# Block 5's first layer by seven products, batch 0 mixed by channel blocks, and values of batch 0 loaded packed, in an attention and low-rank mixer kernel

## The chip, the cores and the metric

The kernel runs on one core of a Trainium2 chip. The metric is the device time of one execution in microseconds (us). Engines are named as in the profile: PE is TensorE (PEld its weight loads), DVE VectorE, ACT ScalarE, POOL GpSimd, SP SyncE. SP, ACT and POOL also issue DMAs; 16 DMA engines move the data of all three.

## The reference

Eight batches of attention with 8 heads of 64 channels, 576 queries, and 592 keys of which the first 16 are "beacons" that every query sees; behind it a mixer over tokens of rank 32, and a two-layer network with ReLU over channels, with a residual:

```python
k_all = np.concatenate([beacon_k, k], axis=2)
v_all = np.concatenate([beacon_v, v], axis=2)
scores = scale * np.matmul(q, k_all.transpose(0, 1, 3, 2))
causal[:, Nb:] = np.triu(np.ones((S, S), dtype=bool), k=1)
scores = np.where(causal, -1000000000.0, scores)
a = np.exp(scores - scores.max(-1, keepdims=True))
a /= a.sum(-1, keepdims=True) + 1e-09
x = np.matmul(a, v_all).transpose(0, 2, 1, 3).reshape(B, S, H * D)
h = x.transpose(0, 2, 1) @ U @ V
u = x + h.transpose(0, 2, 1)
out = u + np.maximum(u @ w_ch1, 0.0) @ w_ch2
```

U is 576x32, V is 32x576, w_ch1 is 512x2048, w_ch2 is 2048x512. All matmuls run in float16 with sums in float32.

## The kernel before

**The work.** Attention goes by pairs of heads: pair p is batch p // 4, heads 2(p % 4) and the next, so there are 32 pairs. The keys and queries of a pair are regrouped on chip (`pr`), turned so that channels lie on partitions (`kT`, `qT`; by PE through a PSUM tile `tps` and two copies, or from batch 3 on by a DMA that transposes, `raw`, and one copy that reorders), and multiplied in four visits a to d (`sps`); after each visit ACT takes the exponential of both heads (`expt`, L321). DVE masks them (L304), PE multiplies with the values `vs` (`po`, 15 matmuls a head, L331), and DVE divides (L340) into `xb`. When the four pairs of a batch are done, the mixer takes `xb`: a product with U (`qtp`, `qts`), then one with V added to x turned, which gives `uT`, channels on partitions, tokens along the row. In the first batches PE turns x by multiplying with the identity (`ups`, L390), later a DMA does (`xt`, L351).

**The blocks.** The 4608 tokens of `uT` go through the network in nine blocks of 512, 0 to 8, which don't line up with the batches of 576: block 0 needs batch 0 alone, block 5 batches 4 and 5, block 8 batch 7. The first layer of a block is 16 chunks of 128 hidden channels (`g_unit`, tile `gps`, L529): four matmuls of 512 columns, one for each 128 input channels cc, and a ReLU into `gT`. Blocks 6, 7 and 8 use instead Strassen's scheme of seven half-sized products (`first_product`, L566): 28 steps of four matmuls of 256 columns, whose sums go by ACT into float32 tiles `hP` (L109) and by DVE into `gT` (L581), after sums of tokens (`token_sum`, `tb`/`tc`) and of weights (`first_sum`, `wf`). The second layer (`product`, L620) has seven products in all blocks; its operands `sT` are sums and differences of quarters of `gT` (`operand_sum`, L601). The scheme needs the second column half of the first eight chunks with the first half taken off; DVE does that while it moves each chunk out of PSUM (L534, and L583 in the seven-product blocks). The result is added to the turned tokens `ut` (transposed by DMA, L520) by DVE (L645) and stored.

**The order.** No scheduler moves anything: `SCRIPT` is a list of some 960 short words, each engine gets the instructions of the words in that order, and each engine's queue runs strictly in order. So a word late in the list can't overtake one before it on the same engine. The words: `G` regroup, `H` cast head rows, `T` turn (the letters that follow name k or q and the engine that copies), `S` a visit of scores and its exponentials, `M` mask, `A` values, `X` mixer, `g` chunk, `F` first-layer product, `V`, `N` and `W` sums of tokens and weights, `p` operand sum, `P` second-layer product, `U`, `x`, `R` transposes by DMA, `k q b v w` loads issued by POOL, and `I1`, one filler matmul of 512 columns on the identity (`idle`, L241). Tiles in PSUM come from one ring of eight, so PE can run at most eight tiles ahead of the engines that empty them. The first loads of batch 0's keys and queries (`load_first`: tiles `stm`, `sth`) are issued by SP and ACT ahead of the list, in float32, and cast on chip.

## Time and profile before

| | |
|---|---|
| median of 3 runs | 341.67 us (340.97 to 342.67) |
| the profiled execution | 341.91 us, of which its span 340.3 us |
| around the span | 1.6 us |
| granted PE clock, mean | 0.999 |
| POOL busy | 103.6 us, 30% of the span |
| DMA moved | 44.17 MB in 135600 packets, 108384 of them under 512 bytes |

The span runs from the first to the last instruction. A busy share counts an instruction from its start to its end; matmuls overlap, so a PE that is always busy can still hold fillers or matmuls that run slower. What one matmul costs is read from how many stand in a stretch of the chain of waits that has no break.

### The profile page before, as it was taken

Reading aid. Unit: us, or ns where it says so; the run is one execution under the profiler, and the core shown is the slowest. Engines: PE = TensorE matmul, PEld = TensorE weight load, DVE = VectorE, ACT = ScalarE, POOL = GpSimd, SP = SyncE. Lnnn points to the kernel's source line nnn. Section 1 sums busy time; section 2 is a strip of 40 time slices with the busy share of each in tenths; the row PEclk is TensorE's granted clock in tenths of the full one; section 3 lists DMA queues with packets and bytes.
Section 4 is the critical chain, followed back from the end, with each engine's and each line's share of the span. In section 5 each row is a group of like instructions: output and inputs, shape, how many; then the busy total and the mean of one; then the engine's idle time right before and its main releaser. Section 6 shows DMA issues by size and latency. Waiting matters only on the chain.

```text
span 340.3 us, 8963 instructions
## 1 busy us (share of the span) xinstructions
PE 330.1 (97%) x3527; PEld 227.9 (67%) x3527; DVE 263.4 (77%) x681; ACT 228.3 (67%) x495; POOL 103.6 (30%) x137
## 2 busy tenths in 40 slices
PE   6989999999999999999999999999999999999994
PEld 2456555684668755775577646765688888888883
DVE  3489687994869766984888768885999999896872
ACT  3779987849787889878886798267912842544500
POOL 7787673070530802360015220000001503303300
PEclk9999999999999999999999999999999999999999
DMA  8999999999999998999969998463445501203023
GB/s 170 237 188 167 126 184 197 118 127 213 159 163 189 163 203 127 128 148 191 183 95 145 175 174 115 33 161 99 48 63 159 85 13 63 77 3 94 3 80 128
DMA packets 135600, 44.17 MB, mean 130 GB/s; under 512 B 108384, under 2 KB 130912, under 8 KB 135552
## 3 DMA queue, kind: packets, MB, share of 16 engines
q0 software_dynamic: 69008, 17.54, 60.1%
q1 hardware_dynamic: 65952, 25.66, 39.9%
q8 instruction: 29, 0.48, 0.6%
q10 hardware_dynamic: 592, 0.34, 0.3%
q14 instruction: 19, 0.16, 0.2%
HBM read 37.63 MB, written 9.44 MB: 138 GB/s over the span
## 4 chain that ended last, share of the span: by engine, by line
PE 84%; DVE 10%; issue 2%; ACT 1%; DMA 1%; ACTq 0%; DVEq 0%
PE gps L529 25%; PE cpY L620 17%; PE cpD L620 9%; PE sps L316 8%; PE po L331 8%; PE cpA L620 4%; PE fpY L566 3%; DVE gT L581 3%; PE idle L241 2%; PE tps L263 2%; PE fpD L566 2%; DVE sT L601 1%; DVE ob L645 1%; DMA sth<-in_beacon_k_dram 1%; PE ups L397 1%
## 5 line engine op out<-in xcount | busy, mean ns | idle before, releaser
L321 ACT ACTIVATE expt<-sps 128x496 f16<-128x496 f32 (+2 forms) x256 | 111.6, 543 | 13.4 <-PE sps L316 11.9
L529 PE MATMUL gps<-uT,w 128*128 128x512 f16 x384 | 91.8, 380 | 0.0
L620 PEld LDWEIGHTS <-gT 128*128 128x128 f16 x576 | 54.6, 98 | 10.5 <-issue 2.3
L529 PEld LDWEIGHTS <-w 128*128 128x128 f16 x384 | 34.3, 98 | 37.1 <-issue 2.4
L587 POOL TENSOR_SCALAR gT<-gT 128x512 f16<-128x512 f16 x12 | 17.8, 1493 | 105.7 <-DVE gT L581 89.1
L620 PEld LDWEIGHTS <-sT 128*128 128x128 f16 x432 | 40.8, 98 | 8.0 <-issue 2.0
L203 POOL DMA_DIRECT2D vs<-in_v_dram x50 | 40.8, 838 | 3.8 <-DMA w<-in_moe_w_ch_dram 1.7
L304 DVE TENSOR_TENSOR expt<-expt,bigmask 128x512 f16<-128x512 f16 x64 | 26.9, 421 | 18.8 <-ACT expt L321 18.8
L331 PEld LDWEIGHTS <-expt 128*128 128x128 f16 (+1 forms) x960 | 35.2, 98 | 8.7 <-DVE expt L304 1.1
L539 ACT ACTIVATE gT<-gps 128x512 f16<-128x512 f32 x48 | 29.3, 618 | 15.4 <-PE gps L529 14.9
L331 PE MATMUL po<-vs,expt 128*128 128x65 f16 (+1 forms) x960 | 37.8, 194 | 0.7 <-DVE expt L304 0.6
L620 PE MATMUL cpY<-wsum,gT 128*128 128x256 f16 x288 | 36.1, 273 | 0.0
L620 PE MATMUL cpD<-w,sT 128*128 128x256 f16 x288 | 35.6, 273 | 0.3 <-DVE sT L601 0.3
L316 PE MATMUL sps<-qT,kT 64*128 64x80 f16 (+4 forms) x384 | 34.3, 284 | 0.2 <-DVE qT L265 0.2
L340 DVE TENSOR_TENSOR xb<-po,rec 128x320 f16<-128x320 f32 x64 | 31.5, 492 | 2.2
L534 DVE SCALAR_TENSOR_TENSOR gT<-gps,gT 128x256 f16<-128x256 f32 x48 | 19.7, 420 | 13.0 <-ACT gT L533 12.9
L109 ACT ACTIVATE hP<-fpY 128x512 f32<-128x512 f32 x24 | 13.7, 597 | 23.1 <-PE fpY L566 22.0
L533 ACT ACTIVATE gT<-gps 128x256 f16<-128x256 f32 x48 | 18.9, 412 | 12.2 <-PE gps L529 11.9
L316 PEld LDWEIGHTS <-kT 64*128 64x128 f16 x384 | 13.8, 94 | 19.8 <-issue 11.1
L645 DVE TENSOR_TENSOR ob<-cpY,ut 128x512 f32<-128x512 f32 (+1 forms) x28 | 18.7, 667 | 5.9 <-PE cpY L620 5.9
L566 PEld LDWEIGHTS <-wf 128*128 128x128 f16 x192 | 18.6, 98 | 3.1 <-issue 0.7
L620 PE MATMUL cpY<-w,gT 128*128 128x256 f16 x144 | 17.7, 273 | 0.0
(118 smaller groups left out, 484.7 us busy)
## 6 DMA issues: line engine op xcount, KB each, us to landing
out_dram<-ob SPq DMA_DIRECT2D x16, 512.0 KB, 4.7
st<-in_k_dram POOLq DMA_DIRECT2D x6, 512.0 KB, 8.0
st<-in_q_dram POOLq DMA_DIRECT2D x6, 512.0 KB, 8.3
vs<-in_v_dram POOLq DMA_DIRECT2D x18, 128.0 KB, 7.9
w<-in_moe_w_ch_dram POOLq DMA_DIRECT2D x4, 512.0 KB, 7.5
w<-in_moe_w_ch_dram POOLq DMA_DIRECT2D x2, 1024.0 KB, 12.0
stm<-in_k_dram SPq DMA_DIRECT2D x4, 256.0 KB, 6.0
out_dram<-ob SPq DMA_DIRECT2D x4, 256.0 KB, 2.8
```

Of the source, the lines that this page charges most:

```text
L203: nc.gpsimd.dma_start(out=dst[a : a + nq[j], j, :, :], in_=src[hs, ds(q0[j], nq[j]), :].rearrange("h p d -> p h d"))
L304: nc.vector.tensor_tensor(out=e4, in0=e4, in1=bigmask, op=ALU.min)
L316: nc.tensor.matmul(ps[i][:, ds(o, w)], kT[hp, c, ds(P * ch, P)], qT[hp, c, ds(qa, w)], start=True, stop=True,)
L321: nc.scalar.activation(out=ex[i][:, ds(PAD + SLOT * g, gw[g])], in_=ps[i][:, 0 : gw[g]], func=AF.Exp, scale=scale)
L331: nc.tensor.matmul(po[:, j, :], ex[0 : nk[c], ds(blk[(c, j)], P)], vs[0 : nk[c], ds(c * H * E + h * E, E)], start=(c == 0), stop=(c == j),)
L340: nc.vector.tensor_tensor(out=xb[:, h // 2, :, ds(D * (h % 2), D)], in0=po[:, :, 0:D], in1=r.broadcast_to([P, NT, D]), op=ALU.mult)
L529: nc.tensor.matmul(g, w1[:, cc, ts(dc, P)], uT[:, cc, ds(ring(t0), 512)], start=(cc == 0), stop=(cc == NCC - 1))
L534: nc.vector.scalar_tensor_tensor(out=gT[:, dc, H2:512], in0=g[:, H2:512], scalar=0.0, in1=gT[:, dc, 0:H2], op0=ALU.max, op1=ALU.subtract,)
L539: nc.scalar.activation(out=gT[:, dc, :], in_=g, func=AF.Relu)
L566: nc.tensor.matmul(ps[:, i, :], a[:, kk, ts(2 * mp + i, P)], b[:, kk, :], start=opens and i == 0 and kk == 0, stop=kk == 1, skip_group_che ...
L620: nc.tensor.matmul(ps[:, i, :], a[:, f, ds(P * i, P)], b[:, f, :], start=opens and i == 0 and f == 0, stop=f == NK - 1, skip_group_check=True,
L645: nc.vector.tensor_tensor(out=out, in0=ps[:, ii, :], in1=other, op=ALU.add)
```

## The change

- **Block 5's first layer** joins blocks 6 to 8 in the seven products: 64 matmuls of 512 columns become 112 of 256.
- **Values of batch 0** (`f`, `packed_loads`): rows 112 to 575 come in one DMA of four tokens per packet into a tile `vf`, the first 112 rows and the beacons in two more, instead of 12 DMAs of one token per packet. PE then picks the rows apart (`D`, `unpack`): four matmuls of 512 columns with a selecting matrix `pick` for each of four key blocks, and a copy into `vs`.
- **Batch 0 is mixed by channel blocks** (`j`, `J`): each cc as soon as its pair of heads is done, its matmuls standing alone instead of four side by side. **Chunks begun ahead** (`h`): four chunks of block 0 issue three of their four matmuls before the fourth channel block stands.
- **Joint turns**: transposes of `uT` and `xb` take two channel blocks in one DMA (18 for 36, and 10 for 20). `uT` is laid out block by block, and every batch's mixer is cut where a block ends.
- **Bulk differences**: every chunk goes out by one ReLU of 512 columns on ACT; DVE takes the first half off in one instruction of 1024 elements per half of the chunks, at `p..0`.
- **ReLU by engine**: in the seven-product blocks the script names the engine (A, V, G) of each ReLU that follows a DVE sum.
- **The script is written anew.** POOL now regroups 24 half pairs from float16 tiles and 5 from float32 (1 and 2 before), and reorders 19 of the transposed tiles (none before). The fillers `I1` go from 37 to 24. The last second-layer products stand in the same order.

The core of the diff:

```diff
+    def packed_loads(src, bsrc, vs, vf):
+        dst = vs[:, :].rearrange("p (c h e) -> p c h e", h=H, e=E)[:, 0, :, 0:D]
+        np_ = (S - nq[0]) // VJ
+        nc.gpsimd.dma_start(
+            out=vf[0:np_], in_=src[:, nq[0] : S, :].rearrange("h (p j) d -> p h (j d)", j=VJ)
+        )
+        nc.gpsimd.dma_start(out=dst[Nb : Nb + nq[0]], in_=src[:, 0 : nq[0], :].rearrange("h p d -> p h d"))
+        beacon_load(nc.gpsimd, bsrc, dst, ALLH)
+
+    def unpack(vf, vs, c, copy):
+        ps = pst([P, H, D], F32, name="vps")
+        n = nq[c]
+        rows = ds(VG * (c - 1), n // VJ)
+        for j in range(VJ):
+            nc.tensor.matmul(
+                ps[0:n], pick[rows, ds(VJ - 1 - j, n)], vf[rows, :, ds(D * j, D)], start=(j == 0), stop=(j == VJ - 1)
+            )
+        copy(out=vs[0:n, :].rearrange("p (c h e) -> p c h e", h=H, e=E)[:, c, :, 0:D], in_=ps[0:n])
...
-        edge = NBR * 512 - ring(u0)
-        cuts = [0, edge if 64 <= edge < S else q0[2], S]
+        cuts = [0, 512 - u0 % 512, S]
...
+        def part_of(cc, copy):
+            rs = ds(R * cc, R)
+            for a, e in zip(cuts, cuts[1:]):
+                n = e - a
+                ups = pst([P, n], F32, name="ups")
...
+                nc.tensor.matmul(
+                    ups, cell["q"][rs, :], Vsb[rs, ds(a, n)], start=False, stop=True, skip_group_check=True
+                )
+                copy(out=ring(u0 + a)[:, cc, ds((u0 + a) % 512, n)], in_=ups)
...
-            if dc < NK:
-                nc.scalar.activation(out=gT[:, dc, 0:H2], in_=g[:, 0:H2], func=AF.Relu)
-                nc.vector.scalar_tensor_tensor(
-                    out=gT[:, dc, H2:512], in0=g[:, H2:512], scalar=0.0, in1=gT[:, dc, 0:H2],
-                    op0=ALU.max, op1=ALU.subtract,
-                )
-            else:
-                nc.scalar.activation(out=gT[:, dc, :], in_=g, func=AF.Relu)
+            if n is not None:
+                begun[dc] = g, n
+                return
+            nc.scalar.activation(out=gT[:, dc, :], in_=g, func=AF.Relu)
...
-                if n == 3:
-                    nc.vector.scalar_tensor_tensor(
-                        out=n3, in0=n3, scalar=0.0, in1=a11, op0=ALU.max, op1=ALU.subtract
-                    )
-                elif n == 2:
-                    nc.gpsimd.tensor_scalar_max(out=out, in0=out, scalar1=0.0)
-                else:
-                    nc.scalar.activation(out=out, in_=out, func=AF.Relu)
+                RELU[eng](out)
...
+            if j == 0:
+                nc.vector.tensor_tensor(out=n3, in0=n3, in1=a11, op=ALU.subtract)
...
-        B I1 GqA0 HqA0 I1 I1 I1 k1A I1 b1 I1 HkV0 GkV0 TkV0 v0A TqA0 Sa0:3 I1 GqG1 u I1 GkV1 TkV1 GkA4
...
+        GqV0 I1 HkA0 I1 u HqV0 B f0 I1 I1 I1 I1 I1 GkG0 I1 I1 TqV0 I1 I1 q1B I1 I1 I1 TkV0 Sc0 I1 s I1
+        Sd0 GkG1 Sa0:3 Sb0 M0.0 M0.1 k1A I1 TkV1 GqG1 DV3 DV4 GkA2 DA2 TqA1 I1 DV1 I1 GqA2 Sd1 b1 Sb1
...
```

**The opening on POOL.** First the rows of POOL's queue behind the constants, in the kernel before (`st`, `hd` are loads of batch 1, `vs` values, `pr` the regrouped pairs of batch 0):

```order
L196 DMA st_191<-in_k_dram 128x4x256
L190 DMA hd_189<-in_k_dram 64x4x64
L193 DMA hd_189<-in_beacon_k_dram 16x8x64
L193 DMA vs_126<-in_beacon_v_dram 16x4x64
L203 DMA vs_126<-in_v_dram 112x4x64
L203 DMA vs_126<-in_v_dram 128x4x64 x3
L203 DMA vs_126<-in_v_dram 80x4x64
L253 CAST pr<-stm 128x512
L741 CAST hd_142<-sth 80x128
```

and in the changed kernel:

```order
L220 DMA vf<-in_v_dram 116x8x256
L223 DMA vs_127<-in_v_dram 112x8x64
L203 DMA vs_127<-in_beacon_v_dram 16x8x64
L282 CAST pr<-stm 128x512
L206 DMA st_234<-in_q_dram 128x4x256
L200 DMA hd_232<-in_q_dram 80x4x64
L282 CAST pr<-stm 128x512
L822 CAST hd_142<-sth 80x128
L206 DMA st_233<-in_k_dram 128x4x256
L200 DMA hd_231<-in_k_dram 64x4x64
L282 CAST pr<-stm 128x512
L822 CAST hd_143<-sth 80x128
```

The packed values now stand first, ahead of every load of batch 1, and casts of the first pairs stand between the loads.

**The packed values on PE.** PE's queue where the turn of pair 1's queries ends, before (`tps` the turned tile, `sps` scores):

```order
L263 MATMUL tps<-ident,pr 128x128
L316 LDWEIGHTS kT_124
L316 MATMUL sps_282<-qT,kT_124 128x208
L316 LDWEIGHTS kT_124
L316 MATMUL sps_283<-qT,kT_124 128x208
L316 LDWEIGHTS kT_124
L316 MATMUL sps_290<-qT,kT_124 128x336
```

and in the change (`vps` is the PSUM tile of the picked rows, `idle` a filler):

```order
L292 MATMUL tps<-ident,pr 128x128
L270 LDWEIGHTS ident
L270 MATMUL idle<-ident 128x512
L231 LDWEIGHTS pick
L231 MATMUL vps<-vf,pick 128x512
```

The pick matmuls shown are those of key block 1; twelve more, for key blocks 3, 4 and 2, stand ahead of this turn. All sixteen stand ahead of pair 1's scores, and PE can't pass them while the packed values are missing.

**The first chunk on ACT.** ACT's queue where block 0 begins, before (`sps` scores, `ups` the mixer's tile, `gps` a chunk):

```order
L321 ACTIVATE expt_122<-sps_738 128x496
L321 ACTIVATE expt_123<-sps_739 128x496
L321 ACTIVATE expt_120<-sps_780 128x208
L321 ACTIVATE expt_121<-sps_781 128x208
L109 ACTIVATE pr<-st_191 128x512
L408 ACTIVATE uT<-ups 128x336 x2
L408 ACTIVATE uT<-ups 128x240 x2
L321 ACTIVATE expt_122<-sps_837 128x496
```

and in the change:

```order
L350 ACTIVATE expt_121<-sps_735 128x464
L350 ACTIVATE expt_122<-sps_736 128x464
L109 ACTIVATE uT<-ups 128x512
L109 ACTIVATE uT<-ups 128x64
L109 ACTIVATE pr<-st_495 128x512
L350 ACTIVATE expt_123<-sps_820 128x496
L350 ACTIVATE expt_124<-sps_821 128x496
L350 ACTIVATE expt_121<-sps_830 128x208
```

Before, ACT copies half of `uT` when 42 exponentials are done; in the change it copies one channel block when 38 are done, and the first chunk's PSUM tile comes free with the exponential that follows, `expt_123<-sps_820`, the 39th.

More of the change, by code (lines that the diff above doesn't have):

```diff
@@ L130, with fill_pick @@
     Vsb = const.tile([P, S], F16, name="Vsb", tag="Vsb")
+    VJ = 4
+    VG = P // VJ
+    pick = const.tile([P, VJ - 1 + P], F16, name="pick", tag="pick")
+    def fill_pick():
+        nc.vector.memset(pick, 0.0)
+        for g in range(VJ):
+            rows = ds(VG * g, VG)
+            nc.vector.tensor_copy(out=pick[rows, VJ - 1 : VJ - 1 + P : VJ], in_=ident[rows, rows])
     ones = const.tile([P, 1], F16, name="ones", tag="ones")
@@ L381, in part @@
             n = e - a
+            seven = [f"F{t}1.0" in SCRIPT.split() for t in range(NBLK)]
+            for t in range(NBLK - NBR):
+                assert 512 * (t + NBR) >= u0 + e or uses[t] == NCC + (32 if seven[t] else NDC), (u0, t)
             ups = [pst([P, n], F32, name="ups") for _ in range(NCC)]
@@ L777, with mix_of @@
     ]
-    def mix_of(b, part):
+    def mix_of(b, part, *args):
         if b not in mixes:
-            head, parts = mix_units(xbs[b], S * b, xts.get(b))
-            mixes[b] = [head] + parts
-            for t in range(NBLK - NBR):
-                assert 512 * (t + NBR) >= S * (b + 1) or uses[t] == NDC + NCC, (b, t)
-        mixes[b][part]()
+            head, parts, *by_channel = mix_units(xbs[b], S * b, xts.get(b))
+            mixes[b] = [head] + parts + by_channel
+        mixes[b][part](*args)
     late = {}
@@ L806, in step @@
                 v_loads(v[b], beacon_v[b], vss[b % 2], hs)
+        elif name == "f":
+            late["f"] = stage.tile([P, H, 4 * D], F16, name="vf", tag="st0")
+            packed_loads(v[0], beacon_v[0], vss[0], late["f"])
+        elif name == "D":
+            unpack(late["f"], vss[0], int(arg[1:]), COPY[arg[0]])
         elif name == "u":
@@ L990 @@
                 safe_head(h, qT, kTs[0], vss[0], xb)
-            head, parts = mix_units(xb, 0, None, False)
+            head, parts, *_ = mix_units(xb, 0, None, False)
             head()
```

211 lines of the change are left out of this document (131 added, 80 removed).

## The prediction

> **What bounds the kernel now.** I read the table of stages first, then the chain of waits, then ACT in order of time up to the first chunk. From the page and the stages (start:end and length, then busy us and instructions of PE, PEld, DVE, ACT, POOL, then the clock, the DMA share and GB/s):
>
> ```profile
> PE 330.1 (97%) x3527; PEld 227.9 (67%) x3527; DVE 263.4 (77%) x681; ACT 228.3 (67%) x495; POOL 103.6 (30%) x137
> 20.00:30.00 10.00, 8.98 (x121) 4.92 (x121) 9.35 (x33) 8.12 (x23) 9.49 (x15) 1.00 1.47 170
> 40.00:60.00 20.00, 20.00 (x266) 11.88 (x264) 15.89 (x52) 16.83 (x42) 11.88 (x16) 1.00 1.54 187
> 240.00:260.00 20.00, 20.00 (x260) 15.32 (x259) 19.65 (x50) 7.95 (x18) 0.00 (x0) 1.00 0.43 57
> 260.00:280.00 20.00, 19.66 (x183) 17.09 (x180) 18.92 (x35) 12.48 (x24) 6.05 (x4) 1.00 0.44 99
> ```
>
> From 40 us on PE has no hole worth naming: time there falls only with matmuls. The first 40 us differ, as the chain of waits shows (start, us, what):
>
> ```profile
> 9.30 0.97 PE idle L241 x2
> 14.55 0.32 PE sps L316 x2
> 15.70 0.75 PE idle L241 x3
> 33.37 0.39 PE qtp L371 x20
> 36.91 0.97 PE gps L529 x4
> 38.15 2.59 PE gps L529 x12
> 294.13 1.75 PE fpY L566 x16
> ```
>
> PE runs fillers until the first chunk starts at 36.91. So the kernel has two parts: a start that ends with the first chunk and is paced by whatever feeds PE, and 340.3 - 36.9 = 303.4 us behind it, paced by PE. What feeds PE at the start is read from ACT in order of time (start, us, operation, count, idle before):
>
> ```profile
> 9.33 1.06 ACT L321 ACTIVATE expt<-sps 128x496 f16<-128x496 f32 x2 [1.09 <-PE sps L316]
> 11.71 1.00 ACT L321 ACTIVATE expt<-sps 128x464 f16<-128x464 f32 x2 [0.81 <-PE sps L316]
> 13.18 1.53 ACT L321 ACTIVATE expt<-sps 128x208 f16<-128x208 f32 x4 [0.46 <-PE sps L316]
> 14.90 1.96 ACT L321 ACTIVATE expt<-sps 128x496 f16<-128x496 f32 x4 [0.18 <-PE sps L316]
> 16.76 1.34 ACT L109 ACTIVATE kT<-tps 128x80 f16<-128x80 f16 x4
> 17.96 0.65 ACT L109 ACTIVATE pr<-st 128x512 f16<-128x512 f16 x1
> 18.48 1.56 ACT L321 ACTIVATE expt<-sps 128x496 f16<-128x496 f32 x4
> 20.29 3.38 ACT L321 ACTIVATE expt<-sps 128x208 f16<-128x208 f32 x8 [0.25 <-PE sps L316]
> 25.30 3.38 ACT L321 ACTIVATE expt<-sps 128x496 f16<-128x496 f32 x8 [1.63 <-PE sps L316]
> 28.49 0.80 ACT L109 ACTIVATE qT<-tps 128x64 f16<-128x64 f16 x2
> 29.07 0.83 ACT L109 ACTIVATE Vsb<-vps 128x288 f16<-128x288 f32 x2
> 29.65 0.86 ACT L109 ACTIVATE qT<-tps 128x64 f16<-128x64 f16 x2
> 30.30 2.11 ACT L321 ACTIVATE expt<-sps 128x496 f16<-128x496 f32 x4
> 32.17 0.75 ACT L109 ACTIVATE pr<-st 128x512 f16<-128x512 f16 x1
> 32.69 2.13 ACT L321 ACTIVATE expt<-sps 128x208 f16<-128x208 f32 x6
> 34.51 0.82 ACT L109 ACTIVATE pr<-st 128x512 f16<-128x512 f16 x1
> 35.17 1.37 ACT L408 ACTIVATE uT<-ups 128x336 f16<-128x336 f32 x4
> ```
>
> From 14.90 to 34.51 ACT does 34 exponentials. Of these 19.6 us, 5.2 go to the other rows (1.34 + 0.65 + 0.80 + 0.83 + 0.86 + 0.75) and 1.9 are idle (0.25 + 1.63), so an exponential with its waits for scores costs 12.5 / 34 = 0.37. ACT is the pace of the start, with DVE at 9.35 of 10 close behind.
>
> **The change part by part.** Sums are made against the profiled execution (341.91, span 340.3, so 1.6 around it); the median shown is 0.24 lower.
>
> *Block 5.* A chunk's matmul of 512 columns costs 2.59 / 12 = 0.216, one of 256 costs 1.75 / 16 = 0.109. 64 x 0.216 = 13.8 become 112 x 0.109 = 12.2: -1.6, in a stretch where PE is the pace.
>
> *The packed values.* They replace 12 loads by three, but now all sit behind one load, and PE picks ahead of pair 1's scores. When it lands is bounded by these rows (two of POOL in order of time, then DMA issues with count, size and median us to landing, of the first 45 us and of the whole):
>
> ```profile
> 1.87 0.95 POOL L196 DMA_DIRECT2D st<-in_k_dram  x1
> 9.11 0.65 POOL L203 DMA_DIRECT2D vs<-in_v_dram  x1 [1.66 <-DMA st<-in_k_dram]
> w<-in_moe_w_ch_dram POOLq DMA_DIRECT2D x1, 1024.0 KB, 10.3
> w<-in_moe_w_ch_dram POOLq DMA_DIRECT2D x2, 1024.0 KB, 12.0
> ```
>
> The load in that place now lands by 9.1 with 256 KB; 1024 KB take 10.3 to 12.0. The packed one has 928 KB (116 x 8 x 256 x 4 bytes) and is issued at 1.87: 9.1 at the earliest, 13.9 at the latest; I take 10.3, the nearer size at the time of the same dense loading, so 12.2. Twelve picks take 2.6 (to 14.8), the turn of pair 1's queries 0.2, its copy on ACT 0.8, and a cast and its head rows that stand next on ACT 0.9: pair 1's first exponential starts near 17.0. If the values land at 13.9 it is 18.7. At 9.1 the eight exponentials of pair 0 decide (3.6 from 9.33, to 12.9), and with the picks partly under them it is 15.5. I keep 9.33 for the very first exponential: five fillers stand between the turns of queries and keys, at 0.25 to 0.49 each, about as long as DVE needs there for the mask, the selecting matrix and the query copy.
>
> *To the first chunk.* From there ACT has 31 exponentials up to the one that frees the first chunk's tile: 31 x 0.37 = 11.5. Beside them stand `Vsb` 0.83, three copies of turned tiles 2.5, one channel block of `uT` (half of the 1152 columns of the 1.37 row) 0.7 and one regrouping 0.75: 4.8. With the same idle of 1.9 the sum is 18.2 and the first chunk starts at 17.0 + 18.2 = 35.2, against 36.9. Bounds: 15.5 + 16.3 with no idle, 31.8; and 18.7 + 18.2 = 36.9.
>
> *What PE does more at the start* lies in its waiting: 16 picks, 3.5; the mixer's first product alone instead of four abreast, 20 x 0.054 - 0.39 = 0.7 (0.054 is a quarter of 0.216); the second alone, at most 1.0. Thirteen fillers less, at 0.25 to 0.49, free 3.2 to 6.4 of PE. If ACT didn't pace the start, the 5.2 would count, less those fillers: about nothing. Standing behind the first chunk now and ahead of it before are two score visits of 0.32: +0.6.
>
> *Edits that I cost at nothing, since PE covers them.* These groups price them (engine, names, count, busy us, mean ns, then idle before):
>
> ```profile
> L534 DVE SCALAR_TENSOR_TENSOR gT<-gps,gT 128x256 f16<-128x256 f32 x48 | 19.7, 420 | 13.0 <-ACT gT L533 12.9
> L601 DVE TENSOR_TENSOR sT<-gT,sT 128x1024 f16<-128x1024 f16 x18 | 12.3, 683 | 0.2
> L587 POOL TENSOR_SCALAR gT<-gT 128x512 f16<-128x512 f16 x12 | 17.8, 1493 | 105.7 <-DVE gT L581 89.1 <-issue 16.5
> L253 POOL COPY pr<-st 128x512 f16<-128x512 f16 x1 | 0.6, 642 | 0.0
> L203 POOL DMA_DIRECT2D vs<-in_v_dram x50 | 40.8, 838 | 3.8 <-DMA w<-in_moe_w_ch_dram 1.7 <-DMA st<-in_k_dram 1.7 <-DMA st<-in_q_dram 0.4
> ```
>
> Bulk differences take 48 x 0.42 = 20 us off DVE and put back 18 x 0.68 = 12. DVE was at 19.65 of 20 just where block 5 ends and the seven products begin, and PE lost 0.3 us there; block 5's twelve added sums now fall somewhat earlier. I take zero; a gain up to 0.3, and a loss up to 2 if they crowd DVE against batch 7's masks. Joint turns and fewer loads shorten queues that PE doesn't wait for: zero, from -0.5 to +0.5. POOL's 19 reordering copies have no row: 0.64 as a plain copy of that size, 1.49 as POOL's costliest instruction of that size; I take 1.1, halfway, and nothing on the path, because POOL is 30% busy.
>
> *Sum.* 35.2 + 303.4 - 1.6 + 0.6 = 337.6 span, 339.2 as an execution, 339.0 as a median. With the bounds of the first chunk, 31.8 and 36.9: 335.6 to 340.7.
>
> **Rivals.**
>
> *No shorter start.* DVE paces it: 9.35 of 10 busy already, and it gets the copies of three picked blocks, the selecting matrix and the small products of the mixer, while POOL takes four casts off it. Against it: the copies come in pieces that fit between its waits for PE. Then the first chunk stays at 36.9 or slips by half a microsecond: 341.0.
>
> *The values land late* (slower). The packed load shares 16 engines with the eight loads of keys and queries. At half its rate it lands at 1.87 + 20.6 = 22.5, and the first chunk moves by 10; nearer, at 17.5, by 5.3: 344.3. From a landing at 14.9 on nothing is gained, from 16.6 on (339.0 + 4.4) it is slower by over 0.5%. Against it: it stands first in its queue.
>
> *GpSimd comes late* (slower). Key copy of pair 17 on POOL stands directly ahead of its scores on PE, and others have only a few chunks of cover. POOL's queue is strictly in order, and a batch's values hold it for five issues of 0.84. If in each of batches 3 to 7 one copy arrives 1.1 after PE wants it, PE loses 5.5: 344.5. It decides once POOL reaches such a copy less than 1.1 before PE reaches the scores. For it speaks this pair of rows of DVE in order of time:
>
> ```profile
> 16.32 0.20 DVE L741 CAST hd<-sth 80x128 f16<-80x128 f32 x1
> 20.53 1.16 DVE L741 CAST hd<-sth 80x128 f16<-80x128 f32 x1
> ```
>
> The same cast takes 0.96 longer while POOL issues loads, so the two engines do get in each other's way. The Trainium skill, page "SBUF — State Buffer", section "SBUF: two separate sides", makes that a rule: the port pair of VectorE and GpSimd is an exclusive lock, and the loser blocks for the whole instruction. By that rule each moved copy could wait for a whole VectorE instruction, and the time would be this rival's; the trace agrees with the direction, in one place. Against it: POOL's long idle times in the groups above.
>
> **How the numbers follow.** The forecast has 0.62; no shorter start 0.18; GpSimd late 0.12; values late 0.08. About 0.5% (1.7 us) is what a measurement can tell from no change. Of the forecast's 0.62, 0.54 lies below 340.0 and 0.08 within 0.5%; of the first rival 0.03 is faster, 0.13 within, 0.02 slower; the others are slower. Faster 0.57, same 0.21, slower 0.22. The forecast's own range is 335.6 to 340.7; to hold 8 in 10 it reaches up to the slower cases: 335.5 to 344.3.
>
> **What would show it.** Right: the first chunk (four matmuls `gps`, line 600) starts at 34 to 36.5; the packed load lands at 11 to 14; pair 1's first exponential starts near 17; PE's time in the second half is 20.0 of 20; block 5's first layer takes 112 matmuls at 0.109. Wrong: ACT idle for over 3 us between 10 and 20 (values late); PE idle in the middle on a `kT` or `qT` copy of POOL (GpSimd late); the first chunk before 33, or idle in the middle that vanishes or appears by more than 2 us.

## The result, and the profile after

The changed kernel takes 365.36 us (median of 4, 363.98 to 366.52) against 341.32 in the same job (340.95 to 342.67): a ratio of 1.0695, 95% interval 1.0638 to 1.0752. The forecast was 339.0, its range 335.5 to 344.3, and slower had a chance of 0.22. The forecast was wrong in sign. In e11 and e16 of the next section the profiled execution was a disturbed, slower one, so their medians and intervals leave it out, no stretch behind is given for them, and e16's rows are of that execution.

The profiled execution took 363.98, its span is 362.2, 21.9 more than before. The place where the prediction cut the kernel in two, the first chunk, divides that loss. From the page of the changed kernel (engines):

```profile
PE 337.3 (93%) x3586; PEld 237.0 (65%) x3586; DVE 274.8 (76%) x660; ACT 221.5 (61%) x472; POOL 145.5 (40%) x182
```

PE's share fell from 97% to 93%: it waits now, and since the matmuls hardly changed, its 7 us more of busy time mean that some ran slower. PE and ACT in order of time (start, us, operation, count, idle before and what ended it):

```profile
10.56 0.59 PE L345 MATMUL sps<-qT,kT 64*128 64x336 f16 x6 [2.85 <-DVE kT L294]
11.19 1.06 ACT L350 ACTIVATE expt<-sps 128x496 f16<-128x496 f32 x2 [5.08 <-PE sps L345]
22.54 1.93 PE L231 MATMUL vps<-vf,pick 32*128 32x512 f16 x12 [6.78 <-DMA vf<-in_v_dram]
24.58 0.60 ACT L109 ACTIVATE vs<-vps 128x512 f16<-128x512 f32 x1 [7.55 <-PE vps L231]
28.17 2.58 ACT L350 ACTIVATE expt<-sps 128x208 f16<-128x208 f32 x6 [1.64 <-PE sps L345]
50.38 1.47 PE L600 MATMUL gps<-uT,w 128*128 128x512 f16 x6
178.74 1.02 PE L600 MATMUL gps<-uT,w 128*128 128x512 f16 x4 [1.75 <-ACT expt L350]
```

The first chunk starts at 50.38, 13.5 later than the 36.85 of before. Behind it stand 362.2 - 50.38 = 311.8 us, 8.4 more than 303.4. So there are two losses, and the first has its cause in the third row: PE waits 6.78 us for `vf`, and ACT 7.55 behind PE. The sign named for the rival "the values land late", ACT idle for over 3 us between 10 and 20, is there. The packed load itself, from the DMA issues of the first 30 us (count, KB each, median us from issue to landing):

```profile
vf<-in_v_dram POOLq DMA_DIRECT2D x1, 464.0 KB, 20.5
```

It was issued at 1.96 and took 20.5 where I had 10.3. What the DMA engines and PE's clock did meanwhile stands in the table of stages (start:end and length, busy us and instructions of PE, PEld, DVE, ACT and POOL, then PE's granted clock, the DMA share, GB/s):

```profile
8.00:9.00 1.00, 0.00 (x0) 0.00 (x0) 0.99 (x2) 0.00 (x0) 1.00 (x4) 1.00 1.67 160
10.00:14.00 4.00, 3.44 (x15) 0.94 (x17) 0.90 (x5) 1.64 (x4) 0.97 (x3) 0.50 1.42 230
18.00:20.00 2.00, 0.00 (x0) 0.00 (x0) 0.00 (x0) 0.00 (x0) 0.00 (x0) 0.50 0.39 54
20.00:22.00 2.00, 0.00 (x0) 0.00 (x0) 0.00 (x0) 0.00 (x0) 0.00 (x0) 0.50 0.41 55
30.00:32.00 2.00, 2.00 (x15) 1.16 (x13) 1.27 (x4) 0.75 (x2) 0.00 (x0) 0.50 1.50 194
34.00:36.00 2.00, 2.00 (x24) 0.92 (x21) 1.97 (x9) 1.56 (x4) 0.58 (x1) 1.00 0.46 64
160.00:180.00 20.00, 18.03 (x191) 10.71 (x188) 12.18 (x28) 12.47 (x27) 11.51 (x15) 1.00 1.40 150
180.00:200.00 20.00, 17.16 (x169) 10.67 (x166) 18.14 (x38) 12.05 (x28) 13.92 (x16) 0.94 1.21 160
200.00:220.00 20.00, 19.27 (x238) 13.44 (x237) 16.18 (x39) 12.52 (x27) 4.81 (x5) 0.98 1.24 150
```

From 18 to 22 us no engine works, all five are at 0.00, and yet the DMA share is 0.39 to 0.41 and 54 to 55 GB/s flow, where 1.42 and 230 were seen with all loads under way. A load that were only last in line would now have nearly all 16 engines to itself, since beside POOL's queue only some small loads of SP still flow (11.5% of the 16 engines from 18 to 22). POOL's queue, which holds it, had 89.0% of the 16 engines from 10 to 14 and has 28.8% here, near the quarter that 4 of them would be. (The share adds up the time of packets that overlap, so it can pass 1.) The rows also show PE's clock: granted at 1.00 up to 9 us, at 0.50 from 10 on, in a first gap of 2.85 us for the keys, and at 1.00 again only by 34, when the wait for values had long ended. What PE had to do in between ran at half speed.

The second loss lies for the most part between 160 and 220, where PE works 18.03, 17.16 and 19.27 of 20 us. In the kernel before it has 20.00 in each of the three:

```profile
160.00:180.00 20.00, 20.00 (x210) 12.33 (x209) 16.26 (x42) 17.14 (x39) 2.59 (x4) 1.00 0.90 139
180.00:200.00 20.00, 20.00 (x214) 12.48 (x212) 16.09 (x46) 14.22 (x30) 8.48 (x11) 1.00 1.60 157
200.00:220.00 20.00, 20.00 (x228) 13.87 (x228) 15.31 (x40) 13.48 (x30) 0.00 (x0) 1.00 0.93 108
```

That is 5.5 of the 8.4 us. The clock column holds more: 0.94 and 0.98 where before had 1.00. In finer stretches the granted clock is 0.88 from 196 to 198, 0.50 to 200 and 0.54 in the next microsecond, so some 3.4 us at half speed, which begin in a hole of PE of 2.84 us that ends at 197.60. That is an estimated 1.7 us more. The rest was not traced. In the chain of waits the loss starts with a load of queries (start, us, what):

```profile
162.76 2.77 POOL vs L213 x4
166.08 11.48 DMA st<-in_q_dram
177.59 0.63 ACT pr L109
178.22 0.48 ACT expt L350
178.74 1.02 PE gps L600 x4
```

POOL issues five loads of values, then batch 6's queries at 166.08; these land at 177.6, ACT has waited for them, and PE for ACT.

### The profile page after: what moved, and what is told of

It reads as the page before. It is cut to its first block, busy times and chain, and to the rows that moved or that the text cites. A ratio compares the mean times of both kernels' runs of the same rounds, so it can differ in the third digit from the quotient of the medians.

```text
span 362.2 us, 9029 instructions
## 1 busy us (share of the span) xinstructions
PE 337.3 (93%) x3586; PEld 237.0 (65%) x3586; DVE 274.8 (76%) x660; ACT 221.5 (61%) x472; POOL 145.5 (40%) x182
## 4 chain that ended last, share of the span: by engine, by line
PE 70%; DVE 14%; DMA 9%; ACT 3%; issue 2%; POOL 1%; DVEq 0%; POOLq 0%
PE gps L600 16%; PE cpY L684 14%; PE cpD L684 9%; PE po L360 7%; PE sps L345 6%; DMA vf<-in_v_dram 6%; PE fpY L635 5%; DVE sT L665 3%; DMA st<-in_q_dram 3%; PE fpD L635 3%; PE cpA L684 3%; DVE gT L650 2%; ACT expt L350 2%; PE fpA L635 1%; DVE gT L663 1%
## 5 line engine op out<-in xcount | busy, mean ns | idle before, releaser
L600 PE MATMUL gps<-uT,w 128*128 128x512 f16 x320 | 77.0, 380 | 1.8 <-ACT expt L350 1.8
L765 POOL TENSOR_SCALAR gT<-gT 128x512 f16<-128x512 f16 x19 | 29.2, 1547 | 87.3 <-DVE gT L650 87.3
L607 ACT ACTIVATE gT<-gps 128x512 f16<-128x512 f32 x80 | 46.8, 650 | 16.1 <-PE gps L600 15.8
L600 PEld LDWEIGHTS <-w 128*128 128x128 f16 x320 | 28.3, 98 | 33.9 <-issue 5.7
L684 PEld LDWEIGHTS <-sT 128*128 128x128 f16 x432 | 42.1, 100 | 11.1 <-issue 4.1
L333 DVE TENSOR_TENSOR expt<-expt,bigmask 128x512 f16<-128x512 f16 x64 | 30.4, 475 | 23.4 <-ACT expt L350 23.2
L684 PE MATMUL cpY<-wsum,gT 128*128 128x256 f16 x288 | 36.4, 273 | 0.0
L213 POOL DMA_DIRECT2D vs<-in_v_dram x40 | 33.0, 843 | 6.4 <-DMA w<-in_moe_w_ch_dram 6.4
L109 ACT ACTIVATE hP<-fpY 128x512 f32<-128x512 f32 x32 | 18.5, 598 | 22.6 <-PE fpY L635 19.8
L282 POOL COPY pr<-st 128x512 f16<-128x512 f16 x24 | 15.5, 660 | 39.8 <-DVE expt L335 11.0
L345 PEld LDWEIGHTS <-kT 64*128 64x128 f16 x384 | 14.1, 95 | 21.2 <-issue 11.1
L635 PEld LDWEIGHTS <-wf 128*128 128x128 f16 x256 | 24.8, 98 | 2.9
L684 PE MATMUL cpY<-wsum,sT 128*128 128x256 f16 x144 | 18.4, 280 | 3.2 <-DVE ob L719 3.0
L635 PEld LDWEIGHTS <-w 128*128 128x128 f16 x192 | 18.6, 98 | 2.8 <-issue 0.6
## 6 DMA issues: line engine op xcount, KB each, us to landing
w<-in_moe_w_ch_dram POOLq DMA_DIRECT2D x2, 1024.0 KB, 11.1
```

What stands on the lines that cost most here:

```text
L213: nc.gpsimd.dma_start(out=dst[a : a + nq[j], j, :, :], in_=src[hs, ds(q0[j], nq[j]), :].rearrange("h p d -> p h d"))
L333: nc.vector.tensor_tensor(out=e4, in0=e4, in1=bigmask, op=ALU.min)
L345: nc.tensor.matmul(ps[i][:, ds(o, w)], kT[hp, c, ds(P * ch, P)], qT[hp, c, ds(qa, w)], start=True, stop=True,)
L600: nc.tensor.matmul(g, w1[:, cc, ts(dc, P)], ring(t0)[:, cc, :], start=(cc == 0), stop=(cc == NCC - 1), skip_group_check=True,)
L607: nc.scalar.activation(out=gT[:, dc, :], in_=g, func=AF.Relu)
L635: nc.tensor.matmul(ps[:, i, :], a[:, kk, ts(2 * mp + i, P)], b[:, kk, :], start=opens and i == 0 and kk == 0, stop=kk == 1, skip_group_che ...
```

## The experiments

Each row is one kernel; "first chunk" is when the first matmul `gps` starts, "behind" is the span less that. The kernel before ran 7 or 11 times in each job, at medians of 341.7 to 342.0; e9, e10 and e13 ran twice, the others four or more times. Each first chunk and each stretch behind is of one execution. The nine runs from e1 to e14 that have the cut in 112 + 4 issue the same instructions up to the first chunk, and yet it starts anywhere from 36.35 to 38.97, so smaller differences in that column say little.

| run | edit, against the changed kernel | median us | ratio to before (95%) | first chunk | behind |
|---|---|---|---|---|---|
| before | | 341.32 | 1 | 36.85 | 303.4 |
| after | the change | 365.36 | 1.064 to 1.075 | 50.38 | 311.8 |
| e1 | packed load as 112 + 4 partitions | 353.41 | 1.028 to 1.036 | 37.97 | 314.5 |
| e9 | packed load as 114 + 2 | 361.25 | 1.047 to 1.065 | 47.01 | 310.5 |
| e3 | values of batch 0 loaded as before | 356.83 | 1.041 to 1.051 | 41.24 | 313.7 |
| e2 | e1, POOL's 19 copies on ACT | 372.76 | 1.088 to 1.098 | 38.97 | 329.6 |
| e8 | e1, POOL's 19 copies on DVE | 369.96 | 1.072 to 1.085 | 36.69 | 332.4 |
| e4 | the kernel before, with these 19 copies on POOL | 345.65 | 1.005 to 1.018 | 35.37 | 308.8 |
| e5 | e1, queries of batch 6 loaded early | 347.05 | 1.012 to 1.021 | 37.04 | 307.0 |
| e10 | these queries early, load uncut | 363.29 | 1.057 to 1.067 | 50.32 | 311.2 |
| e14 | e1, ten loads early | 351.89 | 1.023 to 1.036 | 36.77 | 314.4 |
| e13 | ten loads early, load uncut | 364.89 | 1.061 to 1.075 | 50.72 | 314.0 |
| e6 | e1, small differences | 355.60 | 1.030 to 1.043 | 36.84 | 318.8 |
| e7 | e1, single turns | 356.27 | 1.034 to 1.045 | 36.35 | 318.4 |
| e12 | e5, block 5 by chunks | 348.17 | 1.012 to 1.021 | 38.96 | 308.3 |
| e11 | e5, three key copies on ACT | 345.48 | 1.007 to 1.018 | 38.44 | |
| e15 | e14, three fillers fewer ahead of the first turn | 355.03 | 1.033 to 1.043 | 38.43 | 315.5 |
| e16 | e5, three fillers fewer between the first two turns | 347.23 | 1.013 to 1.020 | 37.16 | |

**e1: the packed load cut in 112 and 4 partitions.**

```diff
-        nc.gpsimd.dma_start(
-            out=vf[0:np_], in_=src[:, nq[0] : S, :].rearrange("h (p j) d -> p h (j d)", j=VJ)
-        )
+        cut = np_ // 16 * 16
+        for a, e in ((0, cut), (cut, np_)):
+            nc.gpsimd.dma_start(
+                out=vf[a:e],
+                in_=src[:, nq[0] + VJ * a : nq[0] + VJ * e, :].rearrange("h (p j) d -> p h (j d)", j=VJ),
+            )
```

> The changed kernel with the packed load of 116 partitions issued as two: 112 partitions, then 4. In the changed kernel the packed load took 20.5 us from issue to landing, and between 18 and 22 us, when all other loads were down, the 16 DMA engines were busy 20% of the time at 27 GB/s. Theory A (few engines: a load whose partitions are not a multiple of 16 is dealt to a few of the 16 DMA engines, here 4): the values land at 10 to 14 instead of 22.5, the picks start before 15, the first chunk starts 9 to 13 us earlier than 50.45, and the time falls by 9 to 13, to 352 to 356. Rival B (the load shares 16 engines with the eight loads of keys and queries and is simply last): cutting it changes nothing, landing stays within 2 us of 22.5 and the time within 2 us of 365.4. On the 9 us lost between 100 and 280 us: if the late start causes them the time falls to 343 to 347; if GpSimd's copies do, to 352 to 356.

The expectation halves two figures: the column is a share already, so it is 0.39 to 0.41 and 54 to 55 GB/s, as quoted above. The DMA issues of the first 30 us:

```profile
vf<-in_v_dram POOLq DMA_DIRECT2D x1, 448.0 KB, 10.2
vf<-in_v_dram POOLq DMA_DIRECT2D x1, 16.0 KB, 9.7
```

The same bytes in the same place, four partitions apart, take 10.2 in place of 20.5. Theory A holds: the time falls by 12.0, the first chunk comes 12.4 earlier, rival B is out. The loss behind the first chunk stays (314.5), so a late start is not its cause.

**e9: cut in 114 and 2**, to see how the number of partitions counts (`cut = np_ - 2`).

> The changed kernel with the packed load cut in 114 and 2 partitions in place of 112 and 4. Theory A, made sharper (a load is dealt to as many DMA engines as the largest number up to 16 that divides its partitions: 4 for 116, 16 for 112, 6 for 114): 114 partitions take about 20.5 x 4 / 6 = 13.7 from issue to landing, against 20.5 and 10.2, so the values land at 15 to 17 and the time lies between the two, at 354 to 361. Rival A' (any load that isn't a multiple of 16 goes to the same four): 20.1 again, 365. Rival A'' (the engines share it to the nearest partition, and 116 was slow for another reason): 10.2, 353.

```profile
vf<-in_v_dram POOLq DMA_DIRECT2D x1, 456.0 KB, 16.9
```

16.9 lies between 10.2 and 20.5: A' and A'' are both out. It is 3.2 more than a time that goes only by the number of engines (4, 6, 16 for 116, 114, 112). With a fixed part, a + b/4 = 20.5 and a + b/16 = 10.2 give b = 54.9 and a = 6.8, and 6 engines 15.9, still 1.0 short. The order of the three is as the rule says, its size only roughly. The Trainium skill, page "DMA: Bandwidth & Descriptors", section "Why a DMA increments its semaphore by 16 and not by 1", states it: a load goes to the largest number of engines up to 16 that divides the slowest dimension on both sides. It adds an exception for some direct copies from GpSimd's queue, which get all 16; by that the load of 116 would have taken near the 10.2 of 112 partitions (an estimate), and the trace shows 20.5.

**e3: the values of batch 0 loaded as before** (`v0A` in the place of `f0`, `v0B` behind the first keys of batch 1, no `D`, no `pick`).

> The changed kernel with the values of batch 0 loaded as before, in twelve loads by head halves, without picks and without the picking matrix; the rest of the change stays. Theory A: PE no longer waits for the values, the first exponential of pair 0 returns from 11.2 to 9 to 10, the first chunk starts at 36 to 40, and the time is 350 to 354, within 3 us of the run with the load cut. Rival B' (the new order of the start is itself slower, whatever the values do): the first chunk stays after 45 and the time above 358.

Both missed: 356.83 and a first chunk at 41.24. PE no longer waits for values, but its chain of waits up to 22 us runs through POOL, with 3.62 us of issues of values, and then through a key load of batch 1 that takes 9.03. Packed values, cut to reach all engines, bring the first chunk 41.24 - 37.97 = 3.3 earlier in this order, outside the spread named above, and the medians and their intervals lie apart the same way. In this order the packing was a gain; its partition count was the loss.

**e2, e8 and e4: who copies the turned tiles.** The letter in `TkG13`, `TqG15` and 17 more words names the engine: A in e2, V in e8; in e4 the kernel before gets G in the same 19 words.

> As the run before (load in 112 and 4 partitions), and the 19 reordering copies of GpSimd go back to ScalarE. Theory C (GpSimd comes late: it waits in order for turned tiles, and the loads queued behind its copies are issued late; this cost about 9 us between 100 and 280 us): the time falls by another 5 to 10 against the run with the load cut alone. Rival D (the middle loss has another cause, the joint turns or the later loads): within 2 us of that run, or slower where ScalarE's exponentials now wait behind the copies.

> The changed kernel with the load cut, and the 19 reordering copies on VectorE in place of GpSimd. On ScalarE they made it 19 us slower, since its exponentials then waited behind them for turned tiles. Theory C: GpSimd issues its loads on time and no longer slows VectorE, and the time falls by 3 to 8. Rival I (whoever copies waits for the same late turned tiles): the wait moves to VectorE, and the time stays or grows by up to 15.

> The kernel before, with the same 19 reordering copies moved to GpSimd as the change has there, and nothing else. Theory C: GpSimd reaches its waits and its loads late, PE gets idle time between 130 and 280 us, and the time grows by 4 to 10, to 345 to 352. Rival D (the copies are harmless, the loss comes from elsewhere): within 1.5 us of 341.3.

Waits of e2 from 95 to 170 us (engine, line, released by: us in total, times, longest):

```profile
PE sps L348 <- ACT gT L610: 11.9, 4, 6.3
ACT qT L109 <- DMA raw<-pr: 6.6, 1, 6.6
ACT kT L109 <- DMA raw<-pr: 5.4, 1, 5.4
```

Theory C fell in the form given: on ACT or DVE the copies cost 19 and 17 us, because there chunks and exponentials stand behind a copy whose tile isn't turned yet (in e8 DVE waits 9.3 us for turned queries and 7.6 for turned keys from 95 to 240 us). Of the three engines POOL is where that waiting is cheapest in this order. But it isn't free: the same words cost the kernel before 3.9 us (e4), just inside what C expected there.

**e5: batch 6's queries loaded directly behind its keys.**

```diff
-        p20.2 Sb18 k6 Sb19 p21.2 TqG21 b6 P21.1 P22.0 TkG21 Sd19 Sc19 M18.0 M19.0 P25.0 P25.1 M18.1
-        GkA24 v5 GkA23 R22 P26.0 P26.1 GqA23 R23 A18.0 P23.0 P22.1 P23.1 g3.3 A18.1 GkV26 q6 Sd20 Sc20
+        p20.2 Sb18 k6 q6 Sb19 p21.2 TqG21 b6 P21.1 P22.0 TkG21 Sd19 Sc19 M18.0 M19.0 P25.0 P25.1 M18.1
+        GkA24 v5 GkA23 R22 P26.0 P26.1 GqA23 R23 A18.0 P23.0 P22.1 P23.1 g3.3 A18.1 GkV26 Sd20 Sc20
```

> The changed kernel with the load cut as in the first run, and the query loads of batch 6 issued directly behind its key loads, ahead of two reordering copies of GpSimd and of batch 5's six value loads. In the first run these queries land at 167.2, ScalarE waits 3.7 us for them and PE 2.8 us behind it. Theory C1 (the load is late because it stands behind copies that wait for turned tiles): that wait goes, PE gains 2 to 3 us around 165, the time falls by 2 to 4 from the first run's 353.4. Rival: the queries are late because their buffer or the DMA engines come free late; nothing moves by more than 1 us there.

POOL of e1 in order of time, ahead of that load:

```profile
139.12 1.16 POOL L323 COPY kT<-raw 128x512 f16<-128x512 f16 x1 [10.12 <-DMA raw<-pr]
141.25 0.88 POOL L206 DMA_DIRECT2D st<-in_k_dram  x1
148.10 1.09 POOL L323 COPY qT<-raw 128x512 f16<-128x512 f16 x1 [5.30 <-DMA raw<-pr]
151.19 4.20 POOL L213 DMA_DIRECT2D vs<-in_v_dram  x5
155.36 0.91 POOL L206 DMA_DIRECT2D st<-in_q_dram  x1
167.26 1.17 POOL L285 COPY pr<-st 128x512 f16<-128x512 f16 x2 [8.64 <-DMA st<-in_q_dram]
```

The keys go out at 141.25. Then POOL waits 5.30 for a turned tile, copies, issues the values, and only at 155.36 the queries; two of its own regroupings then wait for them. With one word moved they go out at 141.8. The time falls by 6.4, over the 2 to 4 expected: PE's wait of 2.80 at 168 goes, as expected, and so does most of a second one. That one is seen on DVE. DVE of e1, at PE's second hole (3.62 us, which ends at 188.02):

```profile
178.30 1.35 DVE L557 TENSOR_TENSOR wf<-w 128x1024 f16<-128x1024 f16 x1
179.56 1.55 DVE L666 TENSOR_TENSOR gT<-gT 128x1024 f16<-128x1024 f16 x1
182.63 1.80 DVE L668 TENSOR_TENSOR sT<-sT,gT 128x1024 f16<-128x1024 f16 x1
188.49 0.68 DVE L668 TENSOR_TENSOR sT<-sT,gT 128x1024 f16<-128x1024 f16 x1
```

and the same operations in e5, with PE behind them:

```profile
173.91 0.68 DVE L557 TENSOR_TENSOR wf<-w 128x1024 f16<-128x1024 f16 x1
174.51 0.69 DVE L666 TENSOR_TENSOR gT<-gT 128x1024 f16<-128x1024 f16 x1
176.70 0.69 DVE L668 TENSOR_TENSOR sT<-sT,gT 128x1024 f16<-128x1024 f16 x1
...
180.81 1.03 PE L687 MATMUL cpY<-wsum,sT 128*128 128x256 f16 x8 [0.80 <-DVE ob L722]
```

In e1 the first three took 1.35 to 1.80 us. POOL, held up until then, made four copies between 178.0 and 184.9, beside these three; from 185.4 to 189.5 it only issued loads, and DVE was back at 0.68. The three lost 0.67 + 0.87 + 1.12 = 2.7 us. It isn't chance: over all of e1, the rows of one such operation with nothing beside it on POOL (50) or only load issues (13) show 0.67 to 0.69 each, and of the 11 beside one of POOL's copies nine show 0.99 to 1.80. In e5 POOL's copies fall beside other work, and PE's hole is 0.80. In e1 the hole also brought the granted clock down, to 0.50 from about 187.4 to 190.8; in e5 it stays at 1.00. Together: 2.80 + 3.62 - 0.80 = 5.6 of waits and an estimated 1.4 of half clock after the hole, 7.0 of the 314.5 - 307.0 = 7.5 between the two profiles. That the two disturb each other is what the Trainium skill, page "SBUF — State Buffer", section "SBUF: two separate sides", says of the port pair they share; the trace agrees, with factors of 2.0 to 2.6.

**e10, e13, e14: is the middle one cause?** In e10 the queries go early with the load uncut; in e13 and e14 `k6 q6 v5`, ten transfers, stand ahead of `TkG19`, the copy that waits 10.12 above, uncut and cut.

> The changed kernel with its load uncut, and only the query loads of batch 6 moved behind the key loads. If the two losses are independent, the time is 365.4 - 6.4 = 359.0, within 2. If the late start made the middle late, more or less than that: outside 356 to 362.

> The changed kernel with its load uncut, and batch 6's key and query loads and batch 5's value loads (10 transfers) moved ahead of GpSimd's reordering copy of pair 19, which waits 9 us for its turned tile. If the middle's loss is loads held behind that copy and its followers: the 6.4 us come back here too, 357 to 361, and PE has no wait for a load or behind one between 155 and 205 us. Rival (the late start itself leaves the middle late in another way): 362 to 365.

> The same move with the load cut in 112 and 4 partitions. If the loads are the whole of it: 345 to 347.5, as with the queries alone, since the values came within 0.2 us of being in time there. Rival (ten transfers ahead of the copy delay the copy itself, and GpSimd comes late to the scores of pair 19): 349 to 353.

The two losses don't add: in e10 the queries are worth 2.1 in the medians and not 6.4, and with two executions the intervals don't tell the 2.1 from nothing. There the chain of waits goes through the next load in POOL's queue, batch 5's values:

```profile
167.34 0.62 PE po L360 x15
167.97 13.37 DMA vs<-in_v_dram
181.39 0.22 PE po L360
181.61 1.71 PE cpY L684 x8
```

Moving all ten ahead took the rival's way: e14 has 351.89, inside its 349 to 353, and e13 364.89. From PE of e14 in order of time:

```profile
142.70 0.78 PE L348 MATMUL sps<-qT,kT 64*128 64x496 f16 x6 [1.73 <-POOL kT L323]
158.72 3.57 PE L603 MATMUL gps<-uT,w 128*128 128x512 f16 x8 [4.01 <-ACT gT L610]
```

The copy comes 1.73 late to the scores of pair 19, which is what the prediction's rival described for pair 17. The second hole ends a chain in which a turned pair takes 10.32 us: from 130 to 165 us the turns `raw<-pr` take 9.1 from issue to landing in e14 and 6.4 in e5 (medians of four). By these figures loads and turns stand in each other's way around 130 to 180 us, though no run separates the two, and each place of the loads that was tried trades one wait for another; e5 has the best of them.

**e6 and e7: bulk differences and joint turns undone.** In e6 `g_unit` takes the difference of each chunk from PSUM again, and `operand_sum` only in blocks 5 to 8; in e7 `turn` and `turn_x` issue two transposes of one channel block.

> The changed kernel with the load cut, and the differences of the chunk blocks made one chunk at a time from the accumulator as before (blocks 0 to 4), not in bulk. In the first run a bulk difference took 1.55 us where GpSimd was at work and 0.68 where it was not, and PE waited 3.6 us at 188 behind a run of such operations on VectorE. Theory E (the bulk differences put a burst on VectorE between the last chunk and the products): the wait at 188 shrinks to under 1.5 us and the time falls by 2 to 5. Rival F (GpSimd's copies and issues slow whatever VectorE does there): the wait stays within 1 us and the time within 2 us, or grows, since VectorE has 8 us more to do.

> The changed kernel with the load cut, and each joint turn of two channel blocks issued as two turns of one. Theory G (joint turns hold the transposing queue longer and make the turned pairs late: between 130 and 200 us a pair took 4.7 us from issue to landing, 3.3 before): the pairs land a microsecond earlier and the time falls by 2 to 5. Rival H (the number of turns is not felt): within 1.5 us of the first run.

Undoing costs 2.2 and 2.9 in the medians, with intervals that still meet that of e1, and 4.3 and 3.9 behind the first chunk in the profiles. In e6 PE's wait at the second hole shrank from 3.62 to 1.4, as theory E has it, and still the time didn't fall. So neither edit is the loss of the middle; whether they are gains the runs don't tell.

**e12: block 5 back to chunks** (`g5.0` to `g5.15` in the places of 16 of the 28 words `F5..`, the rest and the words `V5..` dropped).

> Load cut and query loads early (347.05 us), and block 5's first layer back to 16 chunks of four matmuls, without its four differences of tokens. By the prediction's own term PE has 112 x 0.109 = 12.2 in the one and 64 x 0.216 = 13.8 in the other: the time grows by 1.6, to 348 to 349. Rival K (VectorE's sums for the seven products cost as much as PE saves): within 0.8 of 347.05, or below it.

The medians differ by 1.1, which the intervals don't tell apart. Behind the first chunk it takes 308.3 - 307.0 = 1.3 longer; its start was later by 1.9 for reasons of its own (below). This agrees with the term of 1.6 and doesn't prove it: 1.1 is also near the 0.8 of the rival.

**e11, e15, e16: the last 5 us.**

> Load cut and query loads early (347.05 us), and the reordering copies of the keys of pairs 25, 26 and 27 on ScalarE in place of VectorE. In that run PE's named waits between 180 and 200 us were 0.8 and 0.73 on VectorE, which was busy 17.97 of 20 there, ScalarE 12.05. Theory J (the rest of the loss in the middle is VectorE's load): 1 to 2 us off, 345 to 346. Rival: the copies make ScalarE's exponentials wait for turned tiles, as the 19 did, and the time grows by 1 to 5.

> As the run before, with two fillers in place of five between the turns of the first queries and keys. Over the runs with the cut load the five took 1.2 to 2.3 us, the first exponential began at 9.5 to 11.1 and the first chunk at 36.4 to 39.0. If these fillers set the start: first exponential at 8.5 to 9.7 in this run, first chunk at 36 to 37, and the median 1 to 2 below the run before. Rival (VectorE paces the start, 9.43 of 10 busy between 20 and 30 us): the first chunk does not move by more than 0.5 from 37.

> Load cut and query loads of batch 6 early (347.05 us), with two fillers in place of five between the turns of the first queries and the first keys (the run before took three away ahead of the first turn instead, and the five stayed). Over the runs with the cut load these five took 1.2 to 2.3 us, the first exponential began at 9.5 to 11.1 and the first chunk at 36.4 to 39.0. If the fillers set the start: first exponential at 8.5 to 10.0, first chunk at 35.5 to 37, median 345 to 346.5. Rival (VectorE paces the start behind it, 9.43 of 10 busy between 20 and 30 us): first chunk at 36.5 to 38, median within 1 of 347.

e11's median of 345.48 lies in theory J's 345 to 346, but its interval overlaps that of e5 almost wholly, so J is neither shown nor out; the growth of the rival isn't seen. In e15 the fillers I took away stood ahead of the first turn, not between the turns, so it doesn't test its theory; PE stayed at the slower of two speeds described at the end for longer (its first six score matmuls took 0.59 us, in e14 0.39), and the first chunk came at 38.43. e16 takes away the right ones. Its PE and ACT in order of time:

```profile
6.79 1.06 PE L273 MATMUL idle<-ident 128*128 128x512 f16 x2
9.86 1.06 ACT L353 ACTIVATE expt<-sps 128x496 f16<-128x496 f32 x2 [3.83 <-PE sps L348]
37.16 1.47 PE L603 MATMUL gps<-uT,w 128*128 128x512 f16 x6
```

The first exponential is as early as in the better runs, and the first chunk comes at 37.16, with the median at 347.23 against e5's 347.05. By that the rival holds and the fillers bring no time. The profile is a weaker test: here each filler took 0.53, at the slower speed, with which e11 and e12 have the first exponential at 11.1, so against those it did come 1.3 earlier.

No version of the changed kernel beat the kernel before; e5 and e11 are the nearest, at 0.7 to 2.1% slower. What of e5's 5 us remains is open. In its profiled execution (345.66) the start is level with before (37.04 against 36.85), and 3.6 lie behind the first chunk.

## Why the prediction was wrong, point by point

- **The packed load "lands at 12.2", bounds 9.1 to 13.9.** This step failed, and with it the forecast. It landed at 22.49. The bounds were taken from loads of 128 partitions and compared by bytes; the count of partitions was not a term. With 112 + 4 it landed at 1.86 + 10.2 = 12.1 (e1), the very time forecast for a load that reaches all engines, but by luck. The bytes were misread too: 928 KB counts the float32 source, and the rows it was held against count the float16 tile, as the 464.0 KB of the load's own row shows. On that scale these rows of the kernel before were the nearest:

```profile
w<-in_moe_w_ch_dram POOLq DMA_DIRECT2D x4, 512.0 KB, 7.5
st<-in_k_dram POOLq DMA_DIRECT2D x1, 512.0 KB, 10.1
st<-in_q_dram POOLq DMA_DIRECT2D x1, 512.0 KB, 6.0
```

They give a landing at 7.9 to 12.0. The rival "the values land late" had the landing (22.5) and the wrong reason, the eight loads beside it: from 18 us on little else moved, and it was no faster.
- **Pair 1's first exponential at 17.0.** It started at 28.17, 5.7 behind the landing; in e1, with values at 12.1, at 17.05. That agreement is luck as well: PE reached the picks in e1 only at 13.42 and had no wait for the values, and in e5 the exponential came at 15.65. In both it starts 6.11 behind the very first exponential (10.94 and 9.54), so with the cut load pair 0 is the bound and not the landing, as the forecast has it only for values at 9.1. That the first exponential would stay at 9.33 failed: 11.19, and 9.5 to 11.2 in the runs with the cut load.
- **"To the first chunk", 18.2 more.** Mis-sized: 22.2 in the changed kernel, where PE ran at half clock up to 32, and 20.9 and 21.4 in e1 and e5 at full clock. Of the 3.2 more in e5, ACT's idle time makes 1.6 (3.5 where 1.9 was assumed), and the exponentials with the step to the chunk 2.1 (12.7 for the first 30, or 0.42 each for 0.37, and 0.9 from the last of them to the chunk); the copies took 0.5 less. So even with the values on time the first chunk stays at 36.4 to 39.0, which is the rival "no shorter start". Its reason, DVE as the pace, is likely but not tested: DVE was 9.43 of 10 busy from 20 to 30 us and has the chain of waits from 22.8 to 30.9, but ahead of that the chain goes through a query load of batch 1 (12.54 us) and POOL's regrouping behind it.
- **"303.4 behind the first chunk", less 1.6, plus 0.6.** Measured 311.8. That all moved loads and copies could be costed at nothing, because PE covers them, failed. POOL's copies took 1.14 (keys) and 1.20 (queries) where I took 1.1. But I priced the copies, and what counted was POOL waiting in order for turned tiles, with the next batches' loads behind it. The rival "GpSimd comes late" named the engine and the strict order, and put the loss on PE waiting for a copy; only e14 shows that, 1.73 us. In the changed kernel PE waits behind a load. The pair of casts that spoke for this rival tells nothing: the quick one, 0.20 us at 16.32, stood beside a load issue of POOL too (16.10 to 16.64). What slows DVE is POOL's copies (e5). And no term was set aside for the clock, which PE's holes in the changed kernel brought to 0.50, at the start and again near 198 us.
- **Block 5, -1.6.** Not contradicted: undone, 1.1 in the medians, which the intervals don't tell from nothing (e12).
- **Bulk differences and joint turns, zero.** No loss was found: undone, the medians are 2.2 and 2.9 higher, within the intervals (e6, e7). DVE's load between 180 and 200 us did rise, from 16.09 to 18.14 of 20; POOL's copies beside it lengthened its operations there.

## What to carry to other kernels

Before pricing a load by its bytes, look at its outermost dimension: a row of the profile with another partition count is no bound for it, and, as here, a few partitions split off can halve its time. An engine that only copies and issues transfers is not idle cover when its queue is in order: ask of each instruction that waits there which loads stand behind it and when their data are wanted. Where the profile of the changed kernel shows a wait with the DMA share far below that of the busy stretches (here 0.40 against 1.42), suspect a transfer that is itself narrow, not a busy memory. Where a hole of PE goes, read the granted clock behind it too.

## What the runs showed of the hardware, unexpected

- Gaps of PE cost more than their length: in the changed kernel its granted clock was 0.50 from 10 to 32 us, in e1 1.00 there. It fell in a gap of 2.85 us; in e9, whose PE had nothing to do from 11.8 on, only in the stretch from 16 to 17 (0.81, then 0.50). In the middle the half clock came with holes of 2.84 us (changed kernel, 3.4 us of it), 3.62 (e1, 3.4) and 4.01 (e14, 6.8), but not behind e1's hole of 2.80 at 168; in e5 and the kernel before, which have no such holes, the clock stays at 1.00 up to the last microseconds. The runs don't show what sets that moment.
- At the very start PE's matmuls run at one of two speeds: five fillers of 512 columns took 2.34 us in e1 and 1.32 in e5, with the same instructions up to there. With that the first exponential moved from 10.94 to 9.54. The slower is the speed of the half clock, though the column shows 1.00 in these first microseconds: four turning matmuls (`tps`) took 0.63 at 8.99 in e1, as in e9 at 21.09 with 0.50 granted, and 0.39 at 7.51 in e5. What sets when the full speed comes is open.
- Reordering copies of 128 x 512 took POOL 1.07 us when alone and up to 1.55 when DVE was busy, and DVE's operations of 1024 elements went from 0.68 to 1.35 to 1.80 at the same time: both sides pay. Load issues of POOL left them at 0.67 to 0.69 in e1.
